# A job list that orders five engines' queues: VectorE priced longer beside GpSimd, x loads landing later, and backlog-dependent slack for TensorE's jobs

## The chip, the core and the metric

One core of one Trainium2 chip runs the program. The metric is device time in microseconds (us) of one execution, given as the median of several runs. TensorE (PE) multiplies matrices, VectorE (DVE) and ScalarE (ACT) work element by element, GpSimd (POOL) does too, and SyncE (SP) issues the DMA transfers. Each engine takes its instructions in the order in which the program was written; instructions of different engines wait for each other through semaphores. A lower time is better.

## The reference

Four batches x of 12480 tokens with 128 channels, and 32 inducing vectors I. First two attention steps, h = mab(I, x) and y = mab(x, h), with

```
s = scale * (q @ kv.T);  s = s - s.max(-1);  a = exp(s);  a = a / (a.sum(-1) + 1e-9);  mab = a @ kv
```

Then a feed-forward layer over all 49920 tokens: u = y @ w_in (128 to 2048), g = u * sigmoid(1.702 u), out = g @ w_out (2048 to 128). Everything is single precision.

## The kernel before

The work is laid out with channels on the 128 partitions. A batch's tokens are cut into seven "supers": six of 4 x 512 tokens and a last one of 2 x 96. A block of the feed-forward layer is 512 tokens (one of four parts of a super), or the leftovers of two batches (384 tokens); there are 98 blocks. A block goes through eight "pairs" of 128-wide chunks of the 2048 hidden channels, 784 pairs in all.

A pair takes these steps. TensorE makes the first product into a PSUM tile `ph` (line 799, two matmuls of 512 columns; ring of two `ph`). ScalarE applies gelu into `g` (line 823, ring of three). The rounded part `hi` is made either by ScalarE, a second gelu from `ph` (line 835), or by VectorE, a cast of `g` (line 842); `choose` picks the one with less booked load. VectorE makes the remainder `lo = g - hi` (line 851). `hi` and `lo` have rings of seven (`HELD`). TensorE then makes six second products into `pso` (lines 878 to 880), adding up over the block's eight pairs. ScalarE or VectorE copies `pso` to `ob` (lines 891, 894), and SP stores it (line 863).

What a block multiplies is not y but the attention weights of its tokens, stacked as `st`, with h @ w_in, so the attention of a batch only has to provide the weights and that product. Attention of batch b is spread over the blocks of batch b - 1: loads of xT (line 915) and of x (line 925); scores of two supers at a time on TensorE (line 999, matmuls on line 320); maxima on VectorE, a turn and a spread over partitions (lines 1018, 1034); a "lump" of exponentials on ScalarE (line 1048), which needs another function table than gelu, so a table load before and after; the weighted sum of x on TensorE (line 1088, matmuls on line 339); sums, division and h (lines 1104 to 1128); then, per super, the second scores (line 1201, matmuls on line 328), a transpose and a maximum on VectorE (lines 1178, 1184), a subtraction on GpSimd (line 1190), and again a lump of exponentials (line 1212). Last, `lay_out` makes the stacks of a super, due 24 pairs (`LEAD`) before its first block: sums on VectorE (line 1239), three operations on GpSimd (lines 1251 to 1253: division by the sum, cast, subtraction), two transposes on VectorE (lines 1258, 1261) and the copies to `st` by SP (line 1279).

Batch 0's attention, the splitting of the weights and the first stacks are written out by hand and run before the rest; SP's last instructions there are the first stack copies (line 596). Everything else is put in order by `Plan`, which runs when the program is written and not on the chip. Its threads (`firsts`, `gelus`, `rests`, `seconds`, `lay_out`, `attentions` and what they spawn) yield `Job`s, each with an engine, an estimate `occ` of how long it holds the engine, an estimate `lat` until its result is there, the units it reads and writes, the rings it takes a buffer of, a rank and perhaps a gate. `ready` gives the time at which a job's inputs and buffers are there by these estimates. `step` takes, among the heads of all threads, the job with the earliest start max(engine free, ready), and among equals the lowest rank, writes its instructions, and books the times. So the estimates decide the order in each engine's queue, and nothing else of the plan reaches the chip. All engines are booked as free at the plan's time zero.

`ahead()` is the plan's count of finished pairs: remainders `lo` written minus pairs whose second products are written. `filler` gives VectorE's attention work rank 1 when `ahead()` is at least `AHEAD` (4) and rank 4 otherwise. A lump has a gate: `ahead()` at least `LUMP` (5). The estimates of VectorE and ScalarE are

```
on_act(n)       = 70 + 0.833 n,  latency 215 + 0.833 n
on_dve(n)       = 75 + 1.042 n,  latency 200 + 1.042 n
on_dve_twice(n) = 75 + 0.521 n,  latency 190 + 0.521 n
```

in ns for n elements per partition: for a pair (1024) ScalarE 923, a remainder 1142, a cast 608. A first-product job is booked with 2 x (2.5 + 0.447 x 512) ns. A DMA job lands, by the plan, 1500 ns after the transfers booked so far are through at 0.34 bytes per ps (a load of 1 MB takes 3.08 us of that), and not before 2000 ns; the `lat` given with a DMA job is not used.

Of the kernel before, what the change touches and what calls it, by code (L numbers as in the profile page):

```python
# [75 lines left out]
class Job:  # L76


    def __init__(self, eng, emit, occ, lat, reads=(), writes=(), takes=(), drops=(),
                 joins=(), rank=5, gate=None, table=None, size=0):  # L80
        self.eng, self.emit, self.occ, self.lat = eng, emit, occ, lat
        self.reads, self.writes, self.takes, self.drops = reads, writes, takes, drops
        self.joins, self.rank, self.gate, self.table, self.size = joins, rank, gate, table, size


class Plan:


    SWITCH = 1294.0
    DMA = 2000.0, 0.34  # L90

    def __init__(self):
        self.free = dict.fromkeys(("PE", "ACT", "DVE", "POOL", "SP"), 0.0)
# [13 lines left out]
    def ready(self, job):  # L107
        if job.gate is not None and not job.gate():
            return None
        t = 0.0  # L110
        for u in job.reads:
            if u.ready is None or u.parts > 0:
                return None
            t = max(t, u.ready)
        for u in job.writes:
            if u.ready is None:
                return None
            t = max(t, u.ready, u.done)
        seen = {}
        for ring, _ in job.takes:  # L120
            f = ring.free(seen.get(ring, 0))
            seen[ring] = seen.get(ring, 0) + 1
            if f is None:
                return None
            t = max(t, f)
        return t

    def step(self):
        best = None
        for thread in self.threads:  # L130
            heads = thread[0] if isinstance(thread[0], list) else [thread[0]]
            found = []
            for job in heads:
                r = self.ready(job)
                if r is not None:
                    s = max(self.free[job.eng], r)
                    found.append((s + job.lat, s, job))
            if not found:
                continue
            _, s, job = min(found, key=lambda f: f[0])  # L140
            rank = job.rank() if callable(job.rank) else job.rank
            key = s, rank
            if best is None or key < best[0]:
                best = key, thread, job, s
        if best is None:
            return False
        _, thread, job, s = best
        self.now = max(self.now, s)
        occ = job.occ
        if job.table is not None and job.table != self.table:  # L150
            if self.table is not None:
                occ += self.SWITCH
                s += self.SWITCH
            self.table = job.table
        for ring, u in job.takes:
            ring.take(u)
        job.emit()
        self.free[job.eng] = s + job.occ
        self.load[job.eng] += occ
        end = s + job.lat  # L160
        if job.size:
            self.dma = max(self.dma, s) + job.size / self.DMA[1] / 1e3
            end = max(s + self.DMA[0], self.dma + 1500.0)
        self.log.append((job.eng, s, s + job.occ, job))
        for u in (*job.writes, *job.joins, *(u for _, u in job.takes)):
            u.ready = max(end, u.ready or 0.0)
            u.parts -= 1
        for u in job.reads:
            u.used(end)
        for u in job.drops:  # L170
            u.used(0.0)
        try:
            thread[0] = next(thread[1])
        except StopIteration:
            self.threads.remove(thread)
        return True
# [24 lines left out]
def set_attention_then_moe(ctx: ExitStack, tc, xT, x, indT, w_in, w_out, outT):  # L201
# [574 lines left out]
    def tokens(i):  # L776
        return sum(p[2] for p in work[i // NG][1])

    def filler(rank=1):
        return lambda: (rank if ahead() >= AHEAD else 4, 0)  # L780

    def firsts():
        for i in range(n):
# [19 lines left out]
                counts["F"] = i + 1  # L803

            one_ = 2.5 + 0.447 * tokens(i)
            yield Job("PE", emit, 2 * one_, 2 * one_ + 200, [stu, *hwu], takes=[(r_ph, phs[i])], rank=(1, i))

    chosen = {}

# [95 lines left out]
    def since(i):  # L905
        return lambda: counts["F"] >= i

    def loads_xT(b, some, i0):
        for units, s in some:
            t0, g, w = sups[s]  # L910
            u = units[b, s]
            ring = r_xl if s == NS - 1 else r_xt

            def emit(u=u, t0=t0, g=g, w=w):
                nc.sync.dma_start(u.ap[:, 0:g * w], xT[:, b * N + t0:b * N + t0 + g * w])

            yield Job("SP", emit, 430, 4500, takes=[(ring, u)], rank=(1, b), gate=since(i0), size=g * w * 512)

    def loads_x(b, units, i0):
        for s in range(NS):  # L920
            t0, g, w = sups[s]
            u = units[s]
            for j in range(g):
                def emit(u=u, t0=t0, w=w, j=j):
# [3 lines left out]
                        x[r0:r0 + w, :].rearrange("(k i) c -> i k c", i=32),  # L928
                    )
                yield Job(  # L930
                    "SP", emit, 430, 4500, takes=[(r_xn, u)] if j == 0 else [], joins=[u] if j else [],
                    rank=(1, b), gate=since(i0), size=w * 512,
                )

# [10 lines left out]
    def attention(b):  # L945
# [49 lines left out]
        for v, pair in enumerate(pairs(range(NS))):  # L995
            pas = [Unit() for _ in pair]

            def emit(pair=pair, pas=pas):
# [3 lines left out]
            yield Job(  # L1002
                "PE", emit, visit(pair), visit(pair) + 250, [x_units[b, s] for s in pair], [],
                [(r_pa, pa) for pa in pas], rank=(0, 0), gate=since(i0 + 6 + 8 * v),
            )
            for s, pa in zip(pair, pas):
                plan.spawn(first_out(s, pa))
# [9 lines left out]
        def turn():  # L1017
            pe_.matmul(pa1.ap[0:1, 0:P], mx1, ident, start=True, stop=True)

        yield Job("PE", turn, 500, 700, [m1u], [], [(r_pa, pa1)], rank=(0, 0))  # L1020
        row = psm.tile([1, G, M], F32, tag="row", name="row", bufs=1)

        def rows():
# [9 lines left out]
        def back():  # L1033
            pe_.matmul(pa2.ap[:, 0:1], row.rearrange("p g m -> p (g m)"), one, start=True, stop=True)

        yield Job("PE", back, 450, 650, [rowu], [], [(r_pa, pa2)], rank=(0, 0))
        nmx = psm.tile([P, 1], F32, tag="nmx", name="nmx")

        def least():
# [5 lines left out]
        def first_exponentials(some):  # L1045

            def emit():
# [8 lines left out]
            occ = sum(190 + 0.833 * sups[s][2] for s in some)  # L1056
            return Job(
                "ACT", emit, occ, occ + 150, [nmxu, cleared], [s1[s] for s in some], rank=(0, 0),
                gate=lambda: ahead() >= LUMP, table="exp",
            )  # L1060

        xn = [Unit(parts=sups[s][1]) for s in range(NS)]
# [22 lines left out]
        for v, some in enumerate(pairs(range(NS))):  # L1085

            def emit(some=some, i=i):
# [5 lines left out]
            yield Job(  # L1093
                "PE", emit, visit(some), visit(some) + 250, [aT[s] for s in some] + [xn[s] for s in some],
                [], [] if v else [(r_pa, pah)], joins=[pah] if v else [], rank=(0, 0),
                gate=since(i0 + 50 + 8 * v),
            )
            i += blocks(some)
        hu = psm.tile([P, P], F32, tag="hu", name="hu", bufs=1)
# [12 lines left out]
        def divide():  # L1112
            divided_sums(pad.ap, hu, rsb)

        yield Job("PE", divide, 1000, 1200, [su], [], [(r_pa, pad)], rank=(0, 0))
        hu_ = Unit(99)

        def set_h():
# [12 lines left out]
                    start=True, stop=True,  # L1131
                )

        yield Job("PE", products, 1200, 1400, [hu_], [], [(r_pa, pw_)], rank=(0, 0))

        def round_():
            act.copy(th.ap, pw_.ap)
# [25 lines left out]
    def second(b, *parts):  # L1163
# [3 lines left out]
        for some in parts:  # L1167
# [29 lines left out]
            for pair in pairs(some):  # L1197
                pas = [Unit() for _ in pair]

                def emit(pair=pair, pas=pas):  # L1200
# [2 lines left out]

                yield Job(
                    "PE", emit, visit(pair), visit(pair) + 250, [x2_units[b, s] for s in pair] + [hu_], [],
                    [(r_pa, pa) for pa in pas], rank=(0, 0),
                )
                for s, pa in zip(pair, pas):
                    plan.spawn(out(s, pa, ready[some.index(s)]))
# [6 lines left out]

            occ = sum(95 + 0.833 * sups[s][2] for s in some)

            def lump(some=some, ready=ready, emit=emit, occ=occ):
                yield Job(  # L1220
                    "ACT", emit, occ, occ + 150, ready, [e_units[b, s] for s in some], rank=(0, 0),
                    gate=lambda: ahead() >= LUMP, table="exp",
                )

            plan.spawn(lump())
# [1 line left out]
    def lay_out():  # L1227

        for key in turns[1:]:
# [30 lines left out]
            def turn_l():  # L1260
                dve.transpose(alT.ap[0:q, 0:w], e.ap[0:q, 0:w])  # L1261

            yield Job("DVE", turn_h, *on_dve(w), [ah], [], [(r_2, ahT)], rank=filler())
            yield Job("DVE", turn_l, *on_dve(w), [e], [], [(r_2, alT)], rank=filler())
            for j in range(g):
                if s < NS - 1:
# [65 lines left out]
```

## Time and profile before

| | before |
|---|---|
| median of 3 runs (lowest to highest) | 1635.38 us (1633.41 to 1635.71) |
| profiled execution | 1635.28 us, span 1633.5 us |
| TensorE busy (share of the span) | 1585.5 us (97%) |
| VectorE busy | 1372.3 us (84%) |
| ScalarE busy | 1313.9 us (80%) |
| GpSimd busy | 183.2 us (11%) |
| mean granted TensorE clock | 0.996 of full speed |

The span runs from the first to the last instruction; the execution's own time is 1.8 us longer. TensorE's busy time is a poor measure here: matmuls are pipelined, the end of each is modelled, and one counts as busy for 0.39 us although the next starts 0.23 us later. How many matmuls start in a stretch tells more. In rows of the trace, "x4" behind an operation is how many instructions are merged into the row, and "[0.44 <-ACT hi L835]" is idle time of that engine before it and what ended it. "PEld" is TensorE's row of weight loads, which run ahead of the matmuls.

### The profile page before, as it was taken

To read this page: it belongs to the slowest core of one execution; us is meant where nothing else is said; L and a number is where in the kernel's file an instruction comes from. 1 tells how busy PE (TensorE), PEld (TensorE's weight loads), DVE (VectorE), ACT (ScalarE), POOL (GpSimd) and SP (SyncE) were. 2 spreads that over 40 slices of the span, in tenths; PEclk is the share of its full clock that TensorE was granted. 3 is DMA by queue.
4 is the path that set the end of the run, shared out by engine and by line. 5 is a ranking of instruction groups with operands and counts; after the bars stand their busy time and mean duration, and the time that the engine had idled before them with its cause. 6 is when DMAs were issued, how large, how long until landed. Compare 5 with 4: busy or idle time off the path is not lost. (4 is left out here: it accounts for less than half of the span.)

```text
span 1633.5 us, 21485 instructions
## 1 busy us (share of the span) xinstructions
PE 1585.5 (97%) x7737; PEld 1219.6 (75%) x7737; DVE 1372.3 (84%) x1542; ACT 1313.9 (80%) x1468; POOL 183.2 (11%) x134
## 2 busy tenths in 40 slices
PE   6799999999999999999999999999999999999999
PEld 3467768778787777777777777777788888777777
DVE  7879878988888888878888788798897988888886
ACT  6488968888878878888887887887878888778875
POOL 4411020120200101102000001011120100110100
PEclk9999999999999999999999999999999999999999
DMA  8352932101144383111134273311111101111100
GB/s 337 122 218 86 172 87 65 39 26 39 45 180 138 67 155 104 38 34 33 33 137 144 78 142 78 113 33 33 33 34 43 38 26 40 39 30 36 39 27 20
DMA packets 84250, 129.79 MB, mean 79 GB/s; under 512 B 12400, under 2 KB 50864, under 8 KB 78000
## 3 DMA queue, kind: packets, MB, share of 16 engines
q1 hardware_dynamic: 84144, 128.41, 27.6%
q8 instruction: 62, 1.02, 0.3%
q14 instruction: 44, 0.36, 0.1%
HBM read 74.10 MB, written 25.56 MB: 61 GB/s over the span
## 5 line engine op out<-in xcount | busy, mean ns | idle before, releaser
L851 DVE TENSOR_TENSOR lo<-g,hi 128x1024 fp32r<-128x1024 f32 (+1 forms) x784 | 965.8, 1258 | 137.4 <-ACT hi L835 127.5
L823 ACT ACTIVATE g<-ph 128x1024 f32<-128x1024 f32 (+1 forms) x784 | 800.4, 1032 | 226.2 <-DVE lo L851 132.7
L878 PE MATMUL pso<-hi,wl 128*128 128x512 f32 (+1 forms) x1568 | 619.2, 395 | 0.0
L879 PE MATMUL pso<-lo,wh 128*128 128x512 f32 (+1 forms) x1568 | 616.2, 393 | 0.6 <-DVE lo L851 0.6
L880 PE MATMUL pso<-hi,wh 128*128 128x512 f32 (+1 forms) x1568 | 616.6, 393 | 0.0
L799 PE MATMUL ph<-st,hw 128*128 128x512 f32 x1536 | 479.8, 400 | 8.8 <-ACT hi L835 6.9
L835 ACT ACTIVATE hi<-ph 128x1024 fp32r<-128x1024 f32 (+1 forms) x446 | 456.1, 1034 | 19.4 <-PE pso L880 18.6
L799 PEld LDWEIGHTS ph<-st,hw 128*128 128x128 f32 x1536 | 274.9, 188 | 113.3 <-ACT hi L835 38.9
L878 PEld LDWEIGHTS pso<-hi,wl 128*128 128x128 f32 x1568 | 294.5, 188 | 75.6 <-issue 7.1
L880 PEld LDWEIGHTS pso<-hi,wh 128*128 128x128 f32 x1568 | 294.1, 188 | 69.6
L879 PEld LDWEIGHTS pso<-lo,wh 128*128 128x128 f32 x1568 | 294.3, 188 | 68.8 <-DVE lo L851 1.1
L842 DVE CAST hi<-g 128x1024 fp32r<-128x1024 f32 (+1 forms) x338 | 240.9, 719 | 59.8 <-PE pso L880 44.3
L1251 POOL TENSOR_TENSOR e<-e,sm 128x512 f32<-128x512 f32 x23 | 33.4, 1452 | 1099.8 <-DVE sm L1243 861.5
L891 ACT COPY ob<-pso 128x512 f32<-128x512 f32 (+1 forms) x67 | 39.7, 592 | 30.1 <-PE pso L880 29.8
L1253 POOL TENSOR_TENSOR e<-e,t 128x512 f32<-128x512 f32 x23 | 44.6, 1940 | 1.8
L1191 POOL TENSOR_TENSOR e<-e,m 128x512 f32<-128x512 f32 x22 | 34.9, 1596 | 79.5 <-DVE m L1185 79.5
L320 PE MATMUL pa<-xt,indT_sb 128*32 128x512 f32 x192 | 26.5, 657 | 16.9 <-DMA xt<-in_xT 16.9
L894 DVE COPY ob<-pso 128x512 f32<-128x512 f32 (+1 forms) x31 | 21.2, 685 | 25.7 <-PE pso L880 25.6
L328 PE MATMUL pa<-xt,hT 128*32 128x512 f32 x192 | 25.5, 638 | 3.0 <-DVE e L1178 2.0
L1252 POOL CAST t<-e 128x512 fp32r<-128x512 f32 x23 | 27.0, 1173 | 1.5
L320 PEld LDWEIGHTS pa<-xt,indT_sb 128*32 128x32 f32 x192 | 4.9, 112 | 28.3 <-issue 16.3
L339 PE MATMUL pa<-xn,t 128*32 128x128 f32 (+1 forms) x594 | 19.1, 275 | 1.0 <-DMA xn<-in_x 1.0
(145 smaller groups left out, 464.0 us busy)
## 6 DMA issues: line engine op xcount, KB each, us to landing
xt<-in_xT SPq DMA_DIRECT2D x48, 1024.0 KB, 7.2
out_T<-ob SPq DMA_DIRECT2D x96, 256.0 KB, 2.0
st<-two SPq DMA_DIRECT2D x368, 64.0 KB, 2.0
xn<-in_x SPq DMA_DIRECT2D x72, 256.0 KB, 6.5
hw<-t SPq DMA_DIRECT2D x48, 64.0 KB, 3.9
raw<-in_w_in SPq DMA_DIRECT2D x4, 512.0 KB, 9.0
raw<-in_w_out SPq DMA_DIRECT2D x4, 512.0 KB, 8.4
st<-ahT SPq DMA_DIRECT2D x8, 64.0 KB, 2.0
```

What stands on the lines that cost most here:

```text
L799: pe_.matmul(ph[:, c, at:at + w], u.ap[:, ch % 4 * P:(ch % 4 + 1) * P], st[:, at:at + w], start=True, stop=True,)
L823: act.activation(gs[i].ap[:, :, 0:w], phs[i].ap[:, :, 0:w], AF.Gelu_apprx_sigmoid)
L835: act.activation(his[i].ap[:, :, 0:w], phs[i].ap[:, :, 0:w], AF.Gelu_apprx_sigmoid)
L842: dve.tensor_copy(his[i].ap[:, :, 0:w], gs[i].ap[:, :, 0:w])
L851: dve.tensor_sub(los[i].ap[:, :, 0:w], gs[i].ap[:, :, 0:w], his[i].ap[:, :, 0:w].bitcast(F32))
L878: pe_.matmul(o, wl[:, ch, :], hi, start=(ch == 0), stop=False)
L879: pe_.matmul(o, wh[:, ch, :], lo, start=False, stop=False)
L880: pe_.matmul(o, wh[:, ch, :], hi, start=False, stop=(ch == NCH - 1))
L891: act.copy(ob.ap[:, 0:w], pso.ap[:, 0:w])
L1191: nc.gpsimd.tensor_sub(e3, e3, m2.ap[0:q, 0:k].unsqueeze(2).broadcast_to([q, k, M]))
L1251: nc.gpsimd.tensor_mul(e3, e3, sm.ap[0:q, 0:nb].unsqueeze(2).broadcast_to([q, nb, M]))
L1253: nc.gpsimd.tensor_sub(e.ap[0:q, 0:w], e.ap[0:q, 0:w], ah.ap[0:q, 0:w].bitcast(F32))
```

## The change

Three things change in the plan, and nothing in the operations themselves.

The booking of a VectorE job is lengthened by 0.34 of the part of it that lies before the time at which GpSimd is booked free (`BESIDE`); load, time and result move by it. A DMA job lands not before its `lat`, which now counts; the loads of xT get 7600 ns and those of x 6800 ns in place of 4500; the transfer rate goes from 0.34 to 0.36. A job can have a `slack`, a function whose value is added to the time at which it is ready: `late(least, most)` gives `most` while `ahead()` is at least 4 and `least` otherwise. First products get 0 or 800 ns; attention's jobs on TensorE 600 or 2000 (scores, weighted sum), 600 or 1500 (the four small ones), 300 or 1500 (second scores); the first transpose of `lay_out` 300 or 1200; the second lumps 1500 always. The lumps' gates open also without five pairs: the first ones when 80 first products of the batch before are written, the second ones 32 pairs before the super's first block.

```diff
+    DMA = 0.36
+    BESIDE = 0.34
-    DMA = 2000.0, 0.34
...
-        return t
+        return t + job.slack() if job.slack else t
...
-        self.free[job.eng] = s + job.occ
-        self.load[job.eng] += occ
-        end = s + job.lat
+        more = 0.0
+        if job.eng == "DVE":
+            more = self.BESIDE * max(0.0, min(job.occ, self.free["POOL"] - s))
+        self.free[job.eng] = s + job.occ + more
+        self.load[job.eng] += occ + more
+        end = s + job.lat + more
         if job.size:
-            self.dma = max(self.dma, s) + job.size / self.DMA[1] / 1e3
-            end = max(s + self.DMA[0], self.dma + 1500.0)
+            self.dma = max(self.dma, s) + job.size / self.DMA / 1e3
+            end = max(end, self.dma + 1500.0)
...
+    def late(least, most):
+        return lambda: most if ahead() >= AHEAD else least
...
-            yield Job("PE", emit, 2 * one_, 2 * one_ + 200, [stu, *hwu], takes=[(r_ph, phs[i])], rank=(1, i))
+            yield Job("PE", emit, 2 * one_, 2 * one_ + 200, [stu, *hwu], takes=[(r_ph, phs[i])], rank=(1, i), slack=late(0, 800))
...
-            yield Job("SP", emit, 430, 4500, takes=[(ring, u)], rank=(1, b), gate=since(i0), size=g * w * 512)
+            yield Job("SP", emit, 430, 7600, takes=[(ring, u)], rank=(1, b), gate=since(i0), size=g * w * 512)
...
-                    "SP", emit, 430, 4500, takes=[(r_xn, u)] if j == 0 else [], joins=[u] if j else [],
+                    "SP", emit, 430, 6800, takes=[(r_xn, u)] if j == 0 else [], joins=[u] if j else [],
...
+                slack=late(600, 2000),
...
-        yield Job("PE", turn, 500, 700, [m1u], [], [(r_pa, pa1)], rank=(0, 0))
+        yield Job("PE", turn, 500, 700, [m1u], [], [(r_pa, pa1)], rank=(0, 0), slack=late(600, 1500))
...
-                gate=lambda: ahead() >= LUMP, table="exp",
+                gate=lambda: ahead() >= LUMP or counts["F"] >= i0 + 80, table="exp",
...
-                gate=since(i0 + 50 + 8 * v),
+                gate=since(i0 + 50 + 8 * v), slack=late(600, 2000),
...
-                    [(r_pa, pa) for pa in pas], rank=(0, 0),
+                    [(r_pa, pa) for pa in pas], rank=(0, 0), slack=late(300, 1500),
...
+            due = first_block[b, some[0]] * NG - LEAD - 8
...
-                    gate=lambda: ahead() >= LUMP, table="exp",
+                    gate=lambda: ahead() >= LUMP or counts["F"] >= due, table="exp", slack=lambda: 1500,
...
-            yield Job("DVE", turn_h, *on_dve(w), [ah], [], [(r_2, ahT)], rank=filler())
+            yield Job("DVE", turn_h, *on_dve(w), [ah], [], [(r_2, ahT)], rank=filler(), slack=late(300, 1200))
```

The jobs `back`, `divide` and `products` get `slack=late(600, 1500)` in the same way as `turn`.

## Rows read from the trace of the kernel before

**Rows 1.** Windows: busy us of PE, PEld, DVE, ACT, POOL (instructions); clock, DMA share, GB/s.

```profile
95.00:1605.00 1510.00, 1494.96 (x7085) 1159.06 (x7084) 1283.99 (x1392) 1248.90 (x1376) 140.35 (x99) 1.00 0.26 69
```

**Rows 2.** The same view behind the last attention, and its undisturbed end.

```profile
1300.00:1600.00 300.00, 297.87 (x1274) 236.38 (x1273) 252.61 (x255) 244.20 (x263) 17.06 (x12) 1.00 0.12 34
1550.00:1600.00 50.00, 50.00 (x216) 39.88 (x215) 41.01 (x42) 40.07 (x44) 0.00 (x0) 1.00 0.07 22
```

**Rows 3.** Waits of TensorE and its weight loads: us in total, times, longest us.

```profile
PEld ph L799 <- ACT hi L835: 39.1, 99, 1.3
...
PE pa L328 <- DVE e L1178: 2.0, 2, 1.0
PE pa L1129 <- DVE hT L549: 1.5, 3, 0.7
PE pa L339 <- DMA xn<-in_x: 1.0, 1, 1.0
```

**Rows 4.** Timeline around one GpSimd trio, 1393 to 1399 us: start, length, instruction.

```profile
1393.04 2.08 DVE L842 CAST hi<-g 128x1024 fp32r<-128x1024 f32 x2
1395.05 3.87 DVE L851 TENSOR_TENSOR lo<-g,hi 128x1024 fp32r<-128x1024 f32 x2
...
1394.64 0.96 POOL L1252 CAST t<-e 128x512 fp32r<-128x512 f32 x1
1395.67 2.15 POOL L1253 TENSOR_TENSOR e<-e,t 128x512 f32<-128x512 f32 x1
...
1396.79 1.03 ACT L823 ACTIVATE g<-ph 128x1024 f32<-128x1024 f32 x1 [2.49 <-DVE lo L851]
...
1398.78 0.73 PE L799 MATMUL ph<-st,hw 128*128 128x512 f32 x2 [0.44 <-ACT hi L835]
```

**Rows 5.** Lines 842 and 851 by themselves: ns shortest/median/longest, first and last start.

```profile
L842 DVE CAST hi<-g x338: 547/686/1779, 105.0 to 1622.4; 128x1024 fp32r<-128x1024 f32 x164, 128x768 fp32r<-128x768 f32 x5
...
L851 DVE TENSOR_TENSOR lo<-g,hi x784: 951/1224/2320, 74.4 to 1623.1; 128x1024 fp32r<-128x1024 f32 x192, 128x768 fp32r<-128x768 f32 x4
```

**Rows 6.** Windows of line 851 alone: DVE busy us (instructions), clock, DMA share, GB/s.

```profile
0.00:1149.40 1149.40, 659.53 (x532) 1.00 0.35 99
0.00:1398.00 1398.00, 819.09 (x664) 1.00 0.31 87
```

**Rows 7.** Windows of line 880 alone: PE and PEld busy us (instructions), as above.

```profile
0.00:1149.40 1149.40, 413.97 (x1052) 197.43 (x1053) 1.00 0.35 99
0.00:1398.00 1398.00, 518.46 (x1320) 247.59 (x1320) 1.00 0.31 87
```

**Rows 8.** Timeline of the start, 78 to 91 us: loads, score matmuls, the first GpSimd trio.

```profile
78.39 9.66 SPq L915 DMA_DIRECT2D xt<-in_xT  x6
...
83.23 1.07 PE L320 MATMUL pa<-xt,indT_sb 128*32 128x512 f32 x8 [2.53 <-DMA xt<-in_xT]
85.74 1.93 PE L320 MATMUL pa<-xt,indT_sb 128*32 128x512 f32 x8 [1.44 <-DMA xt<-in_xT]
...
87.41 1.05 POOL L1251 TENSOR_TENSOR e<-e,sm 128x512 f32<-128x512 f32 x1 [2.81 <-DVE sm L1243]
88.53 0.61 POOL L1252 CAST t<-e 128x512 fp32r<-128x512 f32 x1
89.22 1.30 POOL L1253 TENSOR_TENSOR e<-e,t 128x512 f32<-128x512 f32 x1
```

**Rows 9.** The group of line 1251: busy us, mean ns of one, idle before, releasers.

```profile
L1251 POOL TENSOR_TENSOR e<-e,sm 128x512 f32<-128x512 f32 x23 | 33.4, 1452 | 1099.8 <-DVE sm L1243 861.5 <-ACT g L823 191.3 <-PE pso L880 47.0
```

**Rows 10.** One lump on ScalarE's timeline, and the table loads of all lumps.

```profile
1149.39 1.28 ACT L1215 ACT_TABLE_LOAD   x1
...
1152.55 1.28 ACT L835 ACT_TABLE_LOAD   x1
...
L1052 ACT ACT_TABLE_LOAD  x6: 1283/1283/1283, 166.0 to 967.0; - x6
...
L1215 ACT ACT_TABLE_LOAD  x7: 1283/1283/1283, 112.3 to 1162.1; - x7
```

More of the change, by code (lines that the diff above doesn't have):

```diff
@@ L79, in __init__ @@
     def __init__(self, eng, emit, occ, lat, reads=(), writes=(), takes=(), drops=(),
-                 joins=(), rank=5, gate=None, table=None, size=0):
+                 joins=(), rank=5, gate=None, table=None, size=0, slack=None):
         self.eng, self.emit, self.occ, self.lat = eng, emit, occ, lat
@@ L83, in __init__ @@
         self.joins, self.rank, self.gate, self.table, self.size = joins, rank, gate, table, size
+        self.slack = slack
 class Plan:
     SWITCH = 1294.0
-    DMA = 2000.0, 0.34
+    DMA = 0.36
+    BESIDE = 0.34
     def __init__(self):
@@ L1034, in back @@
             pe_.matmul(pa2.ap[:, 0:1], row.rearrange("p g m -> p (g m)"), one, start=True, stop=True)
-        yield Job("PE", back, 450, 650, [rowu], [], [(r_pa, pa2)], rank=(0, 0))
+        yield Job("PE", back, 450, 650, [rowu], [], [(r_pa, pa2)], rank=(0, 0), slack=late(600, 1500))
         nmx = psm.tile([P, 1], F32, tag="nmx", name="nmx")
@@ L1113, in divide @@
             divided_sums(pad.ap, hu, rsb)
-        yield Job("PE", divide, 1000, 1200, [su], [], [(r_pa, pad)], rank=(0, 0))
+        yield Job("PE", divide, 1000, 1200, [su], [], [(r_pa, pad)], rank=(0, 0), slack=late(600, 1500))
         hu_ = Unit(99)
@@ L1132, in products @@
                 )
-        yield Job("PE", products, 1200, 1400, [hu_], [], [(r_pa, pw_)], rank=(0, 0))
+        yield Job("PE", products, 1200, 1400, [hu_], [], [(r_pa, pw_)], rank=(0, 0), slack=late(600, 1500))
         def round_():
@@ L1217, in second, with lump @@
             occ = sum(95 + 0.833 * sups[s][2] for s in some)
-            def lump(some=some, ready=ready, emit=emit, occ=occ):
+            due = first_block[b, some[0]] * NG - LEAD - 8
+            def lump(some=some, ready=ready, emit=emit, occ=occ, due=due):
                 yield Job(
                     "ACT", emit, occ, occ + 150, ready, [e_units[b, s] for s in some], rank=(0, 0),
-                    gate=lambda: ahead() >= LUMP, table="exp",
+                    gate=lambda: ahead() >= LUMP or counts["F"] >= due, table="exp", slack=lambda: 1500,
                 )
```

## Prediction

> **What bounds the kernel.** I read the stretches first: between 95 and 1605 us TensorE is busy 1494.96 of 1510 us, VectorE 1283.99, ScalarE 1248.90 [rows 1]. TensorE is the bound, so only what TensorE loses can be won. The loss hides in its busy time, because a matmul's recorded end is modelled, so I counted matmuls [rows 2]. From 1550 to 1600 us nothing disturbs TensorE and 216 are counted. A window counts whatever it touches, about two at each cut, so the pace is 50 / 214.3 = 0.2333 us, and a pair (2 first products, 6 second ones) takes 1.87 us. From 1300 to 1600 us, behind the last attention, a clean run would show some 1287; there are 1274. The missing 13 are 13 x 0.233 = 3.0 us, and the stretch holds twelve GpSimd instructions: four trios of lines 1251 to 1253.
>
> The waits tell the form of the loss [rows 3]: weight loads of first products wait for ScalarE's second gelu, line 835, 99 times (39.1 us at the loads, which run ahead of the array, so the array loses less). Attention's matmuls wait 2.0 + 1.5 + 1.0 = 4.5 us for VectorE and for x.
>
> The timeline of one trio shows the chain [rows 4]. Two casts of VectorE take 2.08 us and two lo subtractions 3.87 beside GpSimd, where one cast takes 0.686 and one lo 1.224 [rows 5]. The g ring stays full, gelu waits 2.49 us for lo, its ph tile comes free late, and the first products start 0.44 us after the last matmul's recorded end, which itself lies 0.16 past the pace (0.39 - 0.23): 0.60 us lost. All the while finished pairs lie ready: by 1398 us 664 lo had been started and 1320 / 2 = 660 pairs taken [rows 6, 7]. TensorE's order is fixed by the job list, so it cannot take them.
>
> The start is its own case [rows 8]: TensorE waits 2.53 + 1.44 = 4.0 us for the first two loads of batch 1, which SP issues only from 78.39 us.
>
> **The change, term by term.** It adds and removes no instruction that computes; it changes the list's estimates, and so the order on the five queues. The profiled execution took 1635.28 us, its span 1633.5; the median is 0.10 above it, so the sum stands for both.
>
> *A. First products beside GpSimd.* 3.0 us / 4 = 0.76 us a trio; 23 trios are full size [rows 9]: 23 x 0.76 = 17.5 us. Two edits aim at it. BESIDE lengthens a VectorE job by 0.34 of its overlap: 0.34 x 1142 = 388 ns for a lo, 0.34 x 608 = 207 for a cast (`on_dve`, `on_dve_twice`), so 207 + 2 x 388 = 0.98 us for this trio. In the trace lo came 3.87 - 2 x 1.224 = 1.42 us late, the casts 2.08 - 2 x 0.686 = 0.71, together 2.1, of which 0.76 reached TensorE; 1.4 was absorbed. With 0.98 known to the list, 1.1 stays unknown, less than was absorbed. Then first products get 800 ns of slack while the list counts four finished pairs: TensorE takes seconds instead, and the loss shown, 0.60 us, is shorter. Ends: all 17.5 gained, or nothing where the count is under four and the slack 0. The count at 1398 us stands just at four [rows 6, 7], so slack will go on and off around these very places. I take two thirds: **-11.7 us**.
>
> Behind a held first product stands only TensorE's own queue; who waits for it is ScalarE's gelu, so ScalarE idles more. Its cover is 1510 - 1248.9 = 261 us of idle time [rows 1]; if that went, ScalarE would set the pace. The longer VectorE account also moves roundings to ScalarE: at most 0.34 x 140.35 us of GpSimd time x 0.85 (VectorE's busy share) = 41 us [rows 1], and one moved rounding shifts 0.92 + 0.61 by the list's prices: 0 to 27 more on line 835, at most 25 us of ScalarE's 261. Taken at nothing for the span.
>
> *B. Attention's matmuls.* They get slack of 1200 to 2000 ns when the count is four, above the longest single wait of 1.0 us, and 300 or 600 below it. The 6.8 us for the x tiles cover the 1.0 us of line 339. At stake 4.5 us, between 0 and all; I take **-4.0**, since these waits are short against the slack. The longer chain per batch is covered: a block's lay-out starts 24 x 1.87 = 45 us before the block. The turn's slack (line 1258) and the lumps' 1500 ns lie in the same cover; without it the block's first products would start up to 1.5 us late.
>
> *C. First loads.* The list held the second load landed 2 x 3.08 + 1.5 = 7.7 us after the first's start, now 0.43 + 7.6 = 8.0, plus 0.6 of slack: the score matmuls move back by about 1 us. Most of the 4.0 us comes from elsewhere: SP is still issuing the stacks of the start (line 596), while the list has SP free from its beginning. Ends 0 and 4.0; nearest to the list's own shift, **-1.0**. Store and stack landings (2500 and 2100 ns against 2000) feed rings with 15 and 45 us to spare: nothing.
>
> *D. Lumps of exponentials.* A lump may now start without five pairs when its due count comes. I take 0 and price it below.
>
> Sum: 1635.28 - 11.7 - 4.0 - 1.0 = **1618.6 us**.
>
> **Turns against shares.** GpSimd stretches too: its cast and subtraction take 0.96 and 2.15 us in the trio, 0.61 and 1.30 at 88 us [rows 4, 8], and the second lo ends at 1398.92, 1.10 us, one lo, behind GpSimd's last end of 1397.82 [rows 4]. So the engines take turns, and neither is slowed in proportion. By the Trainium skill, SBUF — State Buffer, section "Who interferes with whom", a VectorE instruction with two SBUF inputs and a GpSimd one that reads SBUF share a port pair as an exclusive lock, and the one that comes second is blocked for the other's whole length. By that rule, which these rows bear out, a price in proportion is wrong for each single instruction.
>
> **Rivals.**
> 1. *Turns: the price stays too low.* VectorE can lose GpSimd's own time, 1.05 + 0.61 + 1.30 = 2.96 us a trio [rows 8], against 0.98 in the list. Then 2.0 us stay unknown, 1.4 are absorbed, and 0.6 x 23 = 13 us of A remain, as slack is off below a count of four. For it: rows 4 and the count at the stall. Against it: the trio shown lost 2.1 us, not 2.96, and a stall at four does get slack. A gives 4.2, B 4.0, C 1.0: **1626 us** (1622 to 1632).
> 2. *Lumps starve TensorE (slower).* Holding first products runs the backlog down to four, the gate of five is seldom met, and lumps start at the due count. A lump keeps ScalarE from 1149.39 to 1153.83, 4.4 us [rows 10]; until the next lo there follow gelu 1.03, hi 0.92 and lo 1.22: 7.6 us, less two first products (0.93), which is 4.8 pairs of six seconds (1.40 us). That lump starts with 532 - 1052 / 2 = 6 pairs [rows 6, 7] and is covered. At 3.5 it would cost 1.3 x 1.40 = 1.8 us; 6 + 7 lumps [rows 10] make 23.7 us, more than A to C give: 1618.6 + 23.7 = **1642 us**. It decides below a count of 4.8 at a lump's start. Against it: the due counts (80 pairs into a batch, 32 before the block) are late, and the list has long to reach five first.
> 3. *The wait moves.* Seconds taken earlier meet a lo that isn't done (line 879): the same lateness at another door, **1635 us**, give or take 3. Against it: four pairs in hand are 4 x 1.40 = 5.6 us, more than the 2.1 of a trio.
> 4. *The change does not do what it says*: slack and price hardly shift the order, and the time is that of rival 3. Against it: slack touches every first product.
>
> **How the numbers follow.** Forecast 0.50, rival 1 0.26, rival 2 0.14, rivals 3 and 4 0.10 together, of which 0.08 fall within 0.2% (3.3 us, about what a measurement of this kernel can tell from no change) and 0.02 just slower. Faster: 0.50 + 0.26 = 0.76; same 0.08; slower 0.14 + 0.02 = 0.16. The predicted time is the likeliest case's, 1618.5. Low end: A, B and C in full, 17.5 + 4.5 + 4.0 = 26, and for some 22 single subtractions of attention on GpSimd a third of a trio each, 5.5: 1604, and 3 us for what the count misses: 1601. High end: 1640, almost to rival 2, which holds the rest. The likeliest case's own range is 1604 to 1622.
>
> **What would show it.** Right: in the stretch that answers to 1300 to 1600 us, 1274 matmuls become nearly 1287; the 99 waits for line 835 fall below 50; line 835 runs up to 27 times more often; attention's waits shrink below 1 us; the wait for the first loads stays above 2 us. Rival 1: trios still show stalls of half a microsecond. Rival 2: TensorE waits 1 to 2 us behind each table load, and the count at a lump's start is under 4.8. Rival 3: line 879 waits for lo. I am wrong altogether if the time grows though the waits for line 835 are gone, or if it falls below 1601 us.

## The result, and the profile after

The changed kernel takes 1610.89 us (median of 4 runs, 1610.68 to 1612.12), the one before 1634.39 us beside it (1633.16 to 1635.71): a ratio of 0.9858, interval 0.9841 to 0.9875, 23.5 us or 1.4% faster. The profiled execution took 1610.68 us, its span 1608.7, at a mean clock of 0.997. The forecast was 1618.5 us, its range 1601 to 1640: right in direction and range, short by 7.6 us.

In the kernel after, the first products stand on line 807, gelu on 831, the second gelu `hi` on 843, the cast on 850, `lo` on 859, the second products on 886 to 888, the score matmuls on 325, the second scores on 333, the weighted sum on 344, the GpSimd trio on 1262 to 1264, the loads of xT on 923 and of x on 934.

Windows of the kernel after, as in rows 2 (busy us of PE, PEld, DVE, ACT, POOL with instructions; clock, DMA share, GB/s): behind its last attention, and an undisturbed end.

```profile
1275.00:1575.00 300.00, 299.69 (x1287) 240.53 (x1286) 257.03 (x257) 247.89 (x271) 21.93 (x12) 1.00 0.12 34
1525.00:1575.00 50.00, 50.00 (x217) 40.24 (x216) 41.24 (x41) 39.52 (x43) 0.00 (x0) 1.00 0.08 25
```

The stretch holds four GpSimd trios again (x12), and now 1287 matmuls in place of 1274: what the prediction gave for a clean run. Other versions below show 1290 and 1292 in such a stretch, so up to 5 matmuls, 1.2 us, may still be lost there. Most of what the trios cost TensorE is gone.

The waits of the kernel after, as in rows 3 (us in total, times, longest).

```profile
PEld ph L807 <- ACT hi L843: 9.0, 13, 0.8
...
PE pso L887 <- DVE lo L859: 0.4, 1, 0.4
...
PE pa L325 <- DMA xt<-in_xT: 12.4, 3, 8.0
PE pa L344 <- DMA xn<-in_x: 2.9, 3, 1.1
...
PE pa L333 <- DVE hT L554: 1.0, 1, 1.0
```

The 99 waits for the second gelu are 13. Of attention's waits for VectorE [rows 3] none is left; the one on line 333 belongs to the part written by hand. Second products wait for `lo` once. One wait grew: the weighted sum waits 2.9 us for x, where it was 1.0.

One trio on the timeline of the kernel after, to lay beside rows 4 (start, length, instruction).

```profile
1314.67 6.94 DVE L859 TENSOR_TENSOR lo<-g,hi 128x1024 fp32r<-128x1024 f32 x4
...
1314.89 1.84 POOL L1262 TENSOR_TENSOR e<-e,sm 128x512 f32<-128x512 f32 x1 [55.68 <-DVE sm L1254]
...
1316.60 0.62 PE L807 MATMUL ph<-st,hw 128*128 128x512 f32 x2
...
1318.22 0.39 PE L888 MATMUL pso<-hi,wh 128*128 128x512 f32 x1
...
1318.44 0.62 PE L807 MATMUL ph<-st,hw 128*128 128x512 f32 x2
```

VectorE is as late as before: four `lo` take 6.94 us, 6.94 - 4 x 1.224 = 2.0 us more than alone [rows 5], where the trio before lost 2.1. But the first products start without idle time, 0.22 us after the last second product. The lateness is not removed, it is absorbed: TensorE has taken finished pairs first. The groups of the page say the same of the whole run (busy us, mean ns; idle before, releaser), first after, then before.

```profile
L859 DVE TENSOR_TENSOR lo<-g,hi 128x1024 fp32r<-128x1024 f32 (+1 forms) x784 | 983.7, 1269 | 183.1 <-ACT hi L843 172.5
L831 ACT ACTIVATE g<-ph 128x1024 f32<-128x1024 f32 (+1 forms) x784 | 804.6, 1030 | 231.4 <-PE ph L807 89.8
...
L843 ACT ACTIVATE hi<-ph 128x1024 fp32r<-128x1024 f32 (+1 forms) x456 | 468.2, 1029 | 4.2 <-PE pso L888 4.0
```

```profile
L851 DVE TENSOR_TENSOR lo<-g,hi 128x1024 fp32r<-128x1024 f32 (+1 forms) x784 | 965.8, 1258 | 137.4 <-ACT hi L835 127.5
L823 ACT ACTIVATE g<-ph 128x1024 f32<-128x1024 f32 (+1 forms) x784 | 800.4, 1032 | 226.2 <-DVE lo L851 132.7
...
L835 ACT ACTIVATE hi<-ph 128x1024 fp32r<-128x1024 f32 (+1 forms) x446 | 456.1, 1034 | 19.4 <-PE pso L880 18.6
```

A `lo` takes 1269 ns in the mean, no less than the 1258 of the kernel before; the second gelu runs 456 times, ten more than before. Before, the largest part of gelu's idle time was ended by `lo` (132.7 us); now it is ended by the first products (89.8 us). ScalarE and VectorE have the time: of the span 291 and 245 us are idle (before, 320 and 261).

The start of batch 1 on the timeline after, beside rows 8.

```profile
77.78 11.04 SPq L923 DMA_DIRECT2D xt<-in_xT  x6
...
86.51 1.92 PE L325 MATMUL pa<-xt,indT_sb 128*32 128x512 f32 x16
```

The score matmuls start at 86.51 us in place of 83.23 and wait for nothing: all 4.0 us of the start are won. More was won with them. Behind these waits the kernel before shows a stretch at the lower level of TensorE's clock, 1.2 GHz (window as in rows 1):

```profile
85.70:89.10 3.40, 3.36 (x12) 1.44 (x13) 1.50 (x4) 0.24 (x1) 1.62 (x2) 0.50 1.01 426
```

In the kernel after, the granted clock is 1.00 from 86 to 89 us. 3.4 us at half the clock cost 1.7.

Worked from the rows, the 24.6 us between the two profiled executions are about: 17.5 (trios), 4.0 (start), 1.7 (its clock), 3.5 (attention's waits for VectorE) less 1.9 (x), 24.8 in all. The 17.5 is the loss of four trios before, 3.0 us, taken for all 23; counted over the whole trace it is some 16 (below). So the sum is good to 2 us at best.

### The profile page after: what moved, and what is told of

The parts are those of the page before. It is cut to its first block, busy times and chain, and to the rows that moved or that the text cites. A ratio compares the mean times of both kernels' runs of the same rounds, so it can differ in the third digit from the quotient of the medians.

```text
span 1608.7 us, 21748 instructions
## 1 busy us (share of the span) xinstructions
PE 1574.9 (98%) x7737; PEld 1227.3 (76%) x7737; DVE 1363.5 (85%) x1518; ACT 1317.5 (82%) x1492; POOL 198.6 (12%) x134
## 3 DMA queue, kind: packets, MB, share of 16 engines
q8 instruction: 63, 1.03, 0.3%
## 5 line engine op out<-in xcount | busy, mean ns | idle before, releaser
L859 DVE TENSOR_TENSOR lo<-g,hi 128x1024 fp32r<-128x1024 f32 (+1 forms) x784 | 983.7, 1269 | 183.1 <-ACT hi L843 172.5
L831 ACT ACTIVATE g<-ph 128x1024 f32<-128x1024 f32 (+1 forms) x784 | 804.6, 1030 | 231.4 <-PE ph L807 89.8
L843 ACT ACTIVATE hi<-ph 128x1024 fp32r<-128x1024 f32 (+1 forms) x456 | 468.2, 1029 | 4.2 <-PE pso L888 4.0
L807 PE MATMUL ph<-st,hw 128*128 128x512 f32 x1536 | 461.5, 398 | 2.6 <-DVE hw L569 1.3
L807 PEld LDWEIGHTS ph<-st,hw 128*128 128x128 f32 x1536 | 282.8, 188 | 92.3 <-issue 10.4
L850 DVE CAST hi<-g 128x1024 fp32r<-128x1024 f32 (+1 forms) x328 | 229.6, 704 | 24.8 <-ACT g L831 16.0
L1262 POOL TENSOR_TENSOR e<-e,sm 128x512 f32<-128x512 f32 x23 | 38.7, 1682 | 1001.2 <-DVE sm L1254 792.5
L899 ACT COPY ob<-pso 128x512 f32<-128x512 f32 (+1 forms) x80 | 47.6, 595 | 13.1 <-PE pso L888 13.1
L1200 POOL TENSOR_TENSOR e<-e,m 128x512 f32<-128x512 f32 x22 | 35.0, 1601 | 87.9 <-DVE m L1194 80.2
L1263 POOL CAST t<-e 128x512 fp32r<-128x512 f32 x23 | 32.8, 1424 | 1.5
L325 PEld LDWEIGHTS pa<-xt,indT_sb 128*32 128x32 f32 x192 | 4.9, 113 | 23.5 <-issue 19.0
L344 PEld LDWEIGHTS pa<-xn,t 128*32 128x32 f32 (+1 forms) x594 | 15.5, 109 | 8.0 <-issue 5.0
```

What stands on the lines that cost most here:

```text
L344: pe_.matmul(pa[32 * j:32 * j + 32, 0:P], aT[0:q, kk, :], xn[0:q, kk], start=(i < G), stop=(i >= n - G),)
L807: pe_.matmul(ph[:, c, at:at + w], u.ap[:, ch % 4 * P:(ch % 4 + 1) * P], st[:, at:at + w], start=True, stop=True,)
L831: act.activation(gs[i].ap[:, :, 0:w], phs[i].ap[:, :, 0:w], AF.Gelu_apprx_sigmoid)
L843: act.activation(his[i].ap[:, :, 0:w], phs[i].ap[:, :, 0:w], AF.Gelu_apprx_sigmoid)
L850: dve.tensor_copy(his[i].ap[:, :, 0:w], gs[i].ap[:, :, 0:w])
L859: dve.tensor_sub(los[i].ap[:, :, 0:w], gs[i].ap[:, :, 0:w], his[i].ap[:, :, 0:w].bitcast(F32))
```

## The experiments

Each is timed against the kernel before (1634.5 to 1635.8 us in these groups). The first four undo one part of the change each.

**The price beside GpSimd.**

```diff
-    BESIDE = 0.34
+    BESIDE = 0.0
```

> The changed kernel with BESIDE at 0, so that the list again books VectorE as if GpSimd were not there. Theory S (the first products' slack took the stalls beside GpSimd): 0.6 us of loss per stall fits inside 0.8 us of slack, so little comes back, 1610 to 1615 us, and line 843's waits stay under 30. Theory P (the price took them): the two thirds of term A that I gave to both come back for the most part, 1618 to 1624 us, with trios losing 0.5 us or more again. A third theory, R, that any new order of the queues would have done, expects a time that has nothing to do with the part left out, anywhere from 1605 to 1630, and stalls at other places than trios.

1614.91 us (1614.38 to 1615.0), ratio 0.9873 [0.986, 0.9887]: 4.0 us above the change. The waits for the second gelu are 24 in place of 13, and two waits of attention for VectorE (1.8 us) are back.

**The first products' slack.**

```diff
-            yield Job("PE", emit, ..., rank=(1, i), slack=late(0, 800))
+            yield Job("PE", emit, ..., rank=(1, i))
```

> The changed kernel without the slack of the first products; price, attention's slack, landings and gates stay. Theory S: term A comes back, 1621 to 1628 us, with waits for line 843 near the 99 of before. Theory P: 1609 to 1614 us, few such waits. If both work together, in between, 1614 to 1621. The count of finished pairs at the first products should rise back to about 4.9 from 4.1 whatever the theory.

1620.82 us (1620.15 to 1621.49), 0.991 [0.9896, 0.9924]: 9.9 us above the change. Its waits of weight loads:

```profile
PEld ph L807 <- ACT hi L843: 33.4, 95, 1.5
```

There are 95 waits, in place of 13 (99 in the kernel before), although VectorE is priced as in the change. The price does not keep them away; the slack does. But a wait at the loads is not yet a loss: the last four trios of this run have 23 of them (4.5 us) and still no loss in their stretch.

```profile
1285.00:1585.00 300.00, 299.94 (x1290) 239.16 (x1289) 253.45 (x256) 251.86 (x269) 19.59 (x12) 1.00 0.12 34
```

How much TensorE loses at first products in each run is counted below.

**Attention's slack**: `slack=late(...)` taken from its seven kinds of TensorE job.

> The changed kernel without slack on attention's seven kinds of TensorE jobs (scores, turn, back, weighted sum, divide, products, second scores). Term B of the prediction says these waits were worth 4.5 us before and are gone now: 1614 to 1616 us, with waits of lines 333, 1138 and 1027 for VectorE back at 3 to 5 us. The rival, that the other edits made them early enough anyway, says 1610 to 1612 us and no such waits.

1618.67 us (1615.44 to 1622.24), 0.9898 [0.9882, 0.9913]: 7.8 us above the change, more than either forecast. But the waits for VectorE come to only 1.4 us. The weighted sum (line 344) waits 7.1 us, and the start 1.5 us again. A re-ordering has opened waits for x, which the next run takes up.

**The landing estimates**, back to those of before.

```diff
-    DMA = 0.36
+    DMA = 0.34
...
-            end = max(end, self.dma + 1500.0)
+            end = max(s + 2000.0, self.dma + 1500.0)
```

> The changed kernel with the DMA booking of before (rate 0.34, landing at 2000 ns or when the transfers are through, lat unused). Term C gave the later landings 1 us of the 4.0 us that the first score matmuls waited; the changed kernel has no wait there at all. If the landings did that, 4 us come back and the wait for xt is seen again near 83 us: 1614 to 1616 us. If the slack of 600 ns and the other new order did it, 1610 to 1612 us. The waits for x tiles, 2.9 us now, should grow towards 4 us in either case if the landing estimate matters for them, and stay if the SP queue is what makes them late.

1627.35 us (1626.32 to 1629.14), 0.9953 [0.9939, 0.9966]: 16.5 us above the change, the largest of the four, and from the part that I had priced at 1 us. Its waits of TensorE:

```profile
PE pa L325 <- DMA xt<-in_xT: 13.4, 4, 8.0
PE pa L344 <- DMA xn<-in_x: 7.6, 2, 4.3
...
PE pa L344 <- DVE lo L859: 3.3, 1, 3.3
```

The start's wait did not come back (13.4 against 16.9 us before): term C was not won by the landing estimate of xT. The weighted sum waits 10.9 us in place of 2.9. The timeline of its longest wait, and then windows of that wait and of the stretches behind the two others (columns as above):

```profile
952.04 17.68 SPq L934 DMA_DIRECT2D xn<-in_x  x16
...
960.46 1.08 PE L344 MATMUL pa<-xn,t 128*32 128x128 f32 x32
965.80 1.93 PE L344 MATMUL pa<-xn,t 128*32 128x128 f32 x32 [4.25 <-DMA xn<-in_x]
967.66 2.08 PE L807 MATMUL ph<-st,hw 128*128 128x512 f32 x4
```

```profile
960.00:965.00 5.00, 1.55 (x35) 0.91 (x33) 3.59 (x4) 0.82 (x1) 0.00 (x0) 0.89 1.22 183
965.00:970.00 5.00, 4.20 (x38) 3.36 (x39) 0.00 (x0) 1.03 (x2) 0.00 (x0) 0.50 1.23 184
...
233.40:236.80 3.40, 3.20 (x35) 2.66 (x36) 2.43 (x3) 0.79 (x1) 0.00 (x0) 0.50 1.18 215
578.20:581.60 3.40, 3.40 (x30) 2.53 (x22) 0.00 (x0) 1.05 (x2) 0.00 (x0) 0.50 1.23 185
```

Two weighted sums stand close behind each other in the queue, and the second super's x is not there: 4.25 us idle. Behind it the granted clock is 0.50, the lower level of 1.2 GHz: four first products take from 967.66 to 969.54, 1.9 us in place of 0.93. With the x products, 1.93 in place of 1.08, the wait draws some 2 us of slow clock after it. The two other waits, 3.3 us each, are followed by 3.4 us at 0.50, which cost 1.7 each. The kernel after has no such stretch at its weighted sums. So 8.0 us of added waiting and some 5.5 of slow clock make 13.5 of the 16.5 us; the rest I did not find in single waits.

The last column and the one before it point to the cause: with the DMA engines full (share 1.2), x comes in at 183 GB/s. So does it in the kernel after, while xT comes at 400. Windows of the kernel after, two loads of x, then the loads of xT:

```profile
560.00:566.00 6.00, 6.00 (x28) 4.84 (x27) 4.33 (x7) 5.26 (x11) 0.00 (x0) 1.00 1.03 181
573.00:579.00 6.00, 5.86 (x53) 4.68 (x54) 4.78 (x6) 3.09 (x4) 0.00 (x0) 1.00 1.14 196
79.00:88.00 9.00, 9.00 (x51) 5.78 (x49) 8.97 (x13) 8.57 (x10) 6.24 (x4) 1.00 0.99 400
```

The plan books both at 340 or 360 GB/s. A load of x differs from one of xT in three things: a token's 128 channels are runs of 512 bytes, one load writes 32 partitions and not 128, and it moves 256 KB and not 1 MB. Which of them halves the rate was not tried. The Trainium skill, DMA: Bandwidth & Descriptors, section "Specifications", gives 512 bytes as the size from which transfers reach line rate. Since the partitions and the load's size differ too, these rows neither agree with that nor contradict it; the plan needs the measured rates either way.

**The parts alone, on the kernel before.** Two theories stood: the new landings are worth much in any order, or they only repay what the slack's order costs. First the landings alone (the two lines above the other way round, and the loads' 7600 and 6800 ns).

> The kernel before with the DMA booking of the change alone (rate 0.36, lat counts, 7600 and 6800 ns). The run with the old landings in the changed kernel cost 16.4 us, most of it in three waits of 3 to 4 us for x tiles in the weighted sums. Theory T (these waits exist only in the changed order, where lumps come late and the weighted sums run one behind the other): before had 1.0 us of them, so 1631 to 1635 us here. Rival L (the landings are worth it in any order): 1618 to 1624 us.

1639.02 us (1636.75 to 1641.21), ratio 1.0019 [1.0009, 1.0028]: 3 us slower. The first theory falls. The waits for x are 3.7 us and those for the second gelu 108. The start's waits are all there, 4.2 us:

```profile
83.71 1.07 PE L320 MATMUL pa<-xt,indT_sb 128*32 128x512 f32 x8 [2.83 <-DVE lo L851]
86.18 1.94 PE L320 MATMUL pa<-xt,indT_sb 128*32 128x512 f32 x8 [1.40 <-DMA xt<-in_xT]
```

The price alone:

```diff
+    BESIDE = 0.34
...
+        if job.eng == "DVE":
+            more = self.BESIDE * max(0.0, min(job.occ, self.free["POOL"] - s))
```

> The kernel before with BESIDE alone. In the changed kernel taking the price away cost 4.0 us. If price and slack of the first products stand in for each other, the price alone should be worth more than that here, 6 to 12 us, 1622 to 1628; if its part is its own, 1629 to 1632; under R (any new order would do) the time says nothing and the stalls beside GpSimd are still there. Expected: 1622 to 1630, waits of first products for line 835 between 50 and 99.

1628.28 us (1627.31 to 1629.78), 0.9955 [0.9943, 0.9967]: 7.5 us faster, with 96 waits for the second gelu still there (32.9 us) and a wait of 4.0 us for x. So the gain lies mostly elsewhere. Of attention's 3.5 us of waits for VectorE 0.9 are left, and of the start's 4.0 us 0.7. The last four trios still cost TensorE as much as before. The start on the timeline, and the stretch with these trios (columns as in rows 2):

```profile
85.29 1.06 PE L324 MATMUL pa<-xt,indT_sb 128*32 128x512 f32 x8
87.01 1.06 PE L324 MATMUL pa<-xt,indT_sb 128*32 128x512 f32 x8 [0.66 <-DVE m L1189]
```

```profile
1294.00:1594.00 300.00, 296.79 (x1272) 236.55 (x1271) 252.29 (x252) 247.32 (x268) 17.64 (x12) 1.00 0.12 34
```

The first products' slack, with the lumps' second way out of their gates, without which, by my reading of the list, the plan never again reaches five pairs before some lump and does not end (no run shows this); `Job`'s new field and `late` come with it:

```diff
+            yield Job("PE", emit, ..., rank=(1, i), slack=late(0, 800))
...
+                gate=lambda: ahead() >= LUMP or counts["F"] >= i0 + 80, table="exp",
...
+                    gate=lambda: ahead() >= LUMP or counts["F"] >= due, table="exp",
```

> The kernel before with the slack of 0 or 800 ns on the first products and the two new ways out of the lumps' gates; no price, old landings, no other slack. Theory T: the stalls beside GpSimd go (12 to 18 us gained) and waits of 3 to 4 us for x tiles come (9 to 16 us lost): 1625 to 1637 us, with line 339 waiting 6 to 12 us for x. Rival L, and the theory that the slack alone is the change: 1616 to 1622 us, x waits under 3 us.

1625.32 us (1623.76 to 1625.6), 0.9933 [0.9921, 0.9945]: 10.4 us faster. Its waits, and its stretch with the last four trios (columns as in rows 2):

```profile
PE pa L321 <- DMA xt<-in_xT: 15.6, 6, 8.0
...
PE pa L340 <- DMA xn<-in_x: 3.9, 2, 2.1
PE pa L329 <- DVE e L1182: 3.0, 5, 1.0
...
PEld ph L803 <- ACT hi L839: 5.3, 11, 0.8
```

```profile
1289.00:1589.00 300.00, 300.00 (x1292) 242.05 (x1292) 259.29 (x259) 246.62 (x267) 19.76 (x12) 1.00 0.12 34
```

The slack alone brings the 99 waits down to 11, and the stretch holds 1292 matmuls. But attention's matmuls now wait more for VectorE (line 329: 3.0 us; lines 1022 and 1133 another 3.1) and for x (less than the 6 to 12 us expected), and of the start's 4.0 us 2.6 are left.

The same with the new landings:

```diff
-            yield Job("SP", emit, 430, 4500, ..., size=g * w * 512)
+            yield Job("SP", emit, 430, 7600, ..., size=g * w * 512)
```

and 6800 for x, 0.36 and `max(end, ...)` as in the change.

> The kernel of the run above with the change's landings too. Theory T: the x waits fall back under 4 us and the time comes 8 to 14 us below the run above, 1616 to 1624 us. What is then left against 1610.9 is price (about 4) and attention's slack (about 8), so 1618 to 1623 is the closest guess. If the landings matter in this order no more than in the order before, the time is that of the run above within 2 us.

1628.04 us (1625.78 to 1632.11), 0.9952 [0.9939, 0.9965]: 2.7 us slower than without them. The second theory falls too, as I had put it. The new landings are still too short for x, and each order draws its own lot: x waits of 1.0 us before, 2.6 here, 2.9 after, 2.3 to 10.9 in the others so far.

**The x loads' rate.** If the booked rate of x is the cause, booking x's bytes twice takes its waits away in any order. Twice tried: in the change,

```diff
-                    rank=(1, b), gate=since(i0), size=w * 512,
+                    rank=(1, b), gate=since(i0), size=2 * w * 512,
```

> The changed kernel with the x loads' bytes counted double in the DMA booking, since the rows show 181 to 196 GB/s while x tiles are loaded and 383 to 400 while xT tiles are, against 360 booked for both. Theory X (waits of the weighted sums for x come from this booking): the 2.9 us of line 344 fall below 1 us, 1607 to 1610 us. Rival R (any new order moves such waits about by a few us): 1607 to 1618 us, with other waits in their place.

1608.72 us (1608.06 to 1609.36), 0.9838 [0.9823, 0.9853]: 2.2 us below the change, and the fastest version. And with the old landings:

> The changed kernel with the old DMA booking, as in the run that cost 16.4 us, but with the x loads' bytes counted double; the xT loads stay as in that run. Theory X: the three waits of 3 to 4 us for x and the half-speed clock behind them go, 1609 to 1615 us. If the xT loads or the stores were the cause there: 1622 to 1628 us. Rival R: anything from 1610 to 1628, with waits at other places.

1610.54 us (1610.1 to 1611.14), 0.9848 [0.9832, 0.9865]: all the 16.5 us are back by this one factor (the 0.3 beyond them lie within the ranges). In neither of the two does line 344 wait for x once. What the landing edit of the change was worth in its order was the rate of x.

**The slack at every count.**

```diff
-            yield Job("PE", emit, ..., rank=(1, i), slack=late(0, 800))
+            yield Job("PE", emit, ..., rank=(1, i), slack=lambda: 800)
```

> The changed kernel with 800 ns of slack for first products at every count instead of only from four finished pairs on. If the dependence on the count matters (held back with little in hand, ScalarE runs dry and TensorE follows), slower: 1616 to 1630 us, gelu waits for first products well above the 89.8 us of line 831 and seconds waiting for lo. If the list's own booking keeps TensorE busy anyway: 1609 to 1613 us.

1614.04 us (1612.0 to 1614.95), 0.9869 [0.9854, 0.9884]: 3.1 us slower than the change, between the two forecasts. On its timeline the start's wait is back:

```profile
83.48 1.06 PE L325 MATMUL pa<-xt,indT_sb 128*32 128x512 f32 x8 [1.27 <-DMA xt<-in_xT]
85.97 1.91 PE L325 MATMUL pa<-xt,indT_sb 128*32 128x512 f32 x8 [1.42 <-DMA xt<-in_xT]
```

These 2.7 us and a single 2.2-us wait of first products (at 1010.53 us, 470 `lo` started and 940 / 2 = 470 pairs taken) are enough for the 3.1. Whether the dependence on the backlog is worth anything apart from the start is not settled.

**Attention's slack again, with x booked right**: the edits of the third and the ninth run together.

> The changed kernel with the x loads' bytes counted double and without slack on attention's TensorE jobs. Taking that slack away alone cost 7.8 us, of which the trace gave some 6 us to waits for x in the weighted sums and 2 us to waits for VectorE. Theory X (what attention's slack is worth beyond term B is a cover for the x booking): 1610 to 1613 us, with waits for VectorE of 2 to 4 us and for x under 1 us. If attention's slack is worth 8 us by itself: 1615 to 1619 us.

1610.89 us (1608.96 to 1611.74), 0.985 [0.9834, 0.9867]: some 2.2 us above the same without that edit (the ranges overlap by 0.4 us), not 7.8. Its timeline shows where:

```profile
85.72 1.06 PE L325 MATMUL pa<-xt,indT_sb 128*32 128x512 f32 x8 [0.45 <-DMA xt<-in_xT]
...
88.27 1.06 PE L325 MATMUL pa<-xt,indT_sb 128*32 128x512 f32 x8 [1.48 <-DMA xt<-in_xT]
```

1.9 us at the start, and 0.8 us of waits for VectorE.

## Why the prediction was right in direction and too small

*A (-11.7 taken, some 16 won).* The mechanism of the slack held, and the size failed: the two thirds. To see the whole of it, I add up how late first products start behind the pace of 0.2325 us (those of 512 columns, from 95 us on, behind another product, and later than 0.04 us): 23.3 us before, 7.1 after. My ground for the two thirds was that the count stands at four, so that the slack would go on and off. By the trace it does. Counted over all first products from 95 us on (`lo` started less half the matmuls of line 888), the share that starts with four pairs or more falls from 90% to 46%, the mean from 4.94 to 4.07; and still 13 waits remain of 99. Rival 1 (turns, 13 us left) did not come, though its premise stands: the single prices are as wrong as before, and the run without any price loses only 4.0 us. The two edits that I had put into this term do not do the same. Of the 23.3 us the slack alone leaves 6.7 and the price alone 19.6; the change without the slack has 16.3, without the price 8.9. So it is the slack that takes the stalls. The price alone takes 3.7 us of them, 3.3 at the start and 2.6 of attention's waits, and loses part of it at x. A price by turns, with GpSimd's whole time, was not tried. Nor were the slack of `lay_out`'s transpose and of the second lumps taken apart.

*B (-4.0 taken).* The waits of attention for VectorE are gone (3.5 us), yet x's grew by 1.9, so the term gave some 1.6. Of the 3.5 the attention's slack itself holds 0.8, by the last run; the price alone takes 2.6 of them.

*C (-1.0 taken, 4.0 won, and 1.7 with the clock).* This step failed. I put "the score matmuls move back by about 1 us" and said that the wait would stay above 2 us; they moved back by 3.3 us and it went. I had added the landing's shift to the smallest slack, 600 ns, and took the two for all that orders them. With the old landings no idle time stands at the start, and with the new ones alone all of it does, so the landing estimate was not it. In four runs without attention's slack 1.5 to 2.7 us are there (the third, seventh, eighth and twelfth), but with the price alone, also without that slack, only 0.7; with the first products' slack at every count 2.7. It is the order of several jobs together; the price alone moves the score matmuls back by 2.1 us, to 85.29 us, and yet the change without the price has no such wait. Which job moved them in the change I did not isolate.

*What I did not see.* The landing of x. I gave its 6800 ns the 1.0 us of line 339 [rows 3] and nothing more. But that number belonged to the old order. In the new one the same estimate carries 16.5 us, since any re-ordering can set two weighted sums behind each other while x arrives at half the booked rate. The trace before had it to see: its window from 202 to 207 us, over a load of x, shows 185 GB/s at a DMA share of 1.12, against the 0.34 bytes per ps (340 GB/s) of the plan.

*D and the lumps (rival 2).* Its premise came in part: of thirteen lumps three start with 4.5 pairs, just below its point of 4.8, and two well below it. Windows of lines 859 and 888 alone in the kernel after, up to these lumps:

```profile
0.00:227.00 227.00, 96.81 (x77) 0.98 0.49 161
0.00:1357.40 1357.40, 820.41 (x654) 1.00 0.32 90
```

```profile
0.00:227.00 227.00, 58.76 (x149) 27.94 (x149) 0.98 0.49 161
0.00:1357.40 1357.40, 510.85 (x1301) 244.01 (x1301) 1.00 0.32 90
```

77 - 149 / 2 = 2.5 pairs and 654 - 1301 / 2 = 3.5. The price did not come:

```profile
1357.00:1367.00 10.00, 10.00 (x44) 7.83 (x43) 6.78 (x9) 8.59 (x10) 0.00 (x0) 1.00 0.11 26
```

That stretch begins with the second of these lumps and holds 44 matmuls of the 10 / 0.2333 + 2 = 45 of a clean one: 0.2 us lost, not 1.8. Behind the first, TensorE's only wait up to 236 us is one of 0.76 us, for x. The other eight lumps start with five pairs or more. Rivals 3 and 4 fall with the single wait on line 887 and with the 23.5 us.

## What to carry to other kernels

In a queue whose order is fixed beforehand by estimates, slack on the jobs that meet late inputs can absorb lateness that the estimates get wrong, as long as other work is ready; here it took some 16 us of such stalls where a price in proportion alone took 4. A wait that costs 1 us in one order says nothing of the next order: look at each estimate that the order rests on, and compare a transfer's booked rate with the GB/s of a window over that transfer, for each shape of load by itself. And time every part of such a change both alone and taken away: here the parts' effects (-7.5, -10.4 and +3 alone; 4.0, 9.9 and 16.5 taken away) do not add up.

## What the runs showed of the hardware that was not expected

- Loads of x, of 256 KB in pieces of 512 bytes onto 32 partitions each, came at 181 to 196 GB/s with the DMA engines full (share 1.03 to 1.23); loads of xT, of 1 MB onto 128 partitions, at 383 (before, 79 to 88 us) to 400.
- In the run with the old landings, waits of 3.33, 3.35 and 4.25 us in a busy stream of matmuls were each followed by a granted clock of 0.50 (3.4, 3.4 and about 5 us long), which cost about half as much again as the wait; in the kernel before, two waits of 2.53 and 1.44 us close together were (3.4 us long).
- VectorE's `lo` beside GpSimd is no faster in the changed kernel (2.0 us late for one trio, 2.1 before), and this costs TensorE nothing there.
